# Block sums and token sums of a fused attention and two-layer expert kernel, moved from VectorE to GpSimd

## The chip, the cores and the metric

The kernel runs on one core of a Trainium2 chip. The time is the device time of one execution in microseconds (us), start to end as the runtime measures it. Engines are named as the profile names them: PE is TensorE (PEld its weight loads), DVE is VectorE, ACT is ScalarE, POOL is GpSimd, SP is SyncE, which here only issues DMAs. Every engine works off its own instructions strictly in the order in which they were written for it, and waits for others by semaphores.

## The reference

Attention with a learned position bias over 4 batches, 8 heads, 576 rows and head size 64; its output, 2304 tokens of width 512, goes through two feed-forward stages.

```python
h   = max(max(x @ moe_w1, x @ moe_w2), x @ moe_w3)          # 512 -> 768
x   = h @ moe_w_out                                         # 768 -> 512
out = (sigmoid(x @ w_gate) * (x @ w_val)) @ w_out           # 512 -> 1536 -> 512
```


## The kernel before

All matrices are float32 and are multiplied on PE as pairs of float16 parts: a value f is scaled, its rounded half is the first part, the rest the second, and three products of parts replace one. `halves` writes such a pair: an ACT copy for the first part, and on DVE `scalar_tensor_tensor` (f times scale minus the first part, L1103) for the second. The scale comes from a sum of squares: ACT squares a decoded block (L1117), one small matmul with ones sums it over the partitions (`col_sums`, L566), and DVE makes the scale of it (L1122, L584 to L586). The weights arrive as 64-bit words and are decoded by three DVE instructions (L554 to L556).

The last stage multiplies the tokens by `w_gate` with a seven-product scheme over 2 x 2 blocks. For it, sums and differences of blocks are needed: `pair_weights` makes four sums of the blocks of one sixth of `w_gate` (128 x 256 elements each, one after the other, each but one needing an earlier one), for six sixths i = 0 to 5; `token_sums` makes four sums of the token blocks of one batch (128 x 576 elements each), for four batches. All of them are written by `add2` (L1096), between SBUF buffers, in float32. `add2` serves a third place too, `quad`, where it makes the second float16 part of the gated product. `quad(b, i)` (which first scales its sigmoid's factor, L1263) are the products of batch b with sixth i (PE L1269), `outs` the last products (PE L1325); `moe1` is the first feed-forward stage (PE L945, its maxima on DVE L975, and its own float16 second parts on DVE L987 or on POOL L986).

Nothing of the order is left to the hardware. The program is recorded instruction by instruction (`Recorder.add`), with a cost for each by engine and size (`Recorder.cost`), and `Recorder.emit` then lays the instructions out engine by engine: it takes next what can start earliest by these costs, within four classes of urgency. An instruction recorded on two engines within one `join` goes to the engine where it would end earlier. So a change of one instruction's engine changes its cost in the plan, and with it the order on all engines. The plan knows no work of one engine that slows another.

The stretch that the change touches runs from the end of attention to the first `outs`: at the profile's times, from 540 to about 708 us the weights of the last stage are decoded and split, the tokens of batches 0 and 1 are prepared, and PE runs the last `moe1` and then the first six `quad`s. One block of sums, that of i = 0, is made earlier (412 to 425 us, in attention).

Of the kernel before, what the change touches and what calls it, by code (L numbers as in the profile page):

```python
# [15 lines left out]
ALU = mybir.AluOpType  # L16
# [400 lines left out]
SIDE_H, FIRST_H = (2, 4), (3, 2)  # L417
SIDE_CLS = ATT
EARLY = 120
ADD_POOL = False  # L420
AHEAD = ()
SPLIT5 = True
PE_ALL, PE_SQ = 6, 8
# [30 lines left out]
def tile_kernel(ctx, tc, q, k, v, w1, b1, w2, mw1, mw2, mw3, mwo, gw, vw, ow, xtab, masks, out):  # L454
# [15 lines left out]
    nc = Recorder(tc.nc, {x.tensor.name for x in (junk[:, :], q, k, v, w1, b1, w2, mw1, mw2, mw3, mwo, gw, vw, ow, xtab, masks, out)})  # L470
# [118 lines left out]
    def copy_psum(dst, src, scale=1.0):  # L589

        with nc.join():
            nc.scalar.activation(dst, src, AF.Copy, scale=scale)  # L592
            nc.vector.tensor_scalar(dst, src, scale, None, op0=ALU.mult)
# [23 lines left out]
    for rv in (rvb0, rvb):  # L617
# [25 lines left out]
        op=ALU.mult,  # L643
# [448 lines left out]

    def add2(dst, a, b, op):

        with nc.join():
            nc.vector.tensor_tensor(dst, a, b, op=op)  # L1096
            if ADD_POOL:
                nc.gpsimd.tensor_tensor(dst, a, b, op=op)

    def halves(dst, f, s):  # L1100

# [3 lines left out]
    def pair_weights(i, raw, F, S4, js=(0, 1), step=128, SW=SW):  # L1105
# [18 lines left out]
        for j, f in zip(js, fs):  # L1124
            W, s = SW[i][j], scl_gv[:, 0, i, j:j + 1]
            if j:
                for h in range(2):
                    halves([W[:, 2 * h:2 * h + 2, e] for e in range(2)], f[:, :, 128 * h:128 * h + 128].rearrange("p (o k) f -> p o k f", o=2), s)
                    yield
                continue  # L1130
            t = S4().rearrange("p (o k f) -> p o k f", o=4, k=2)
            a11, a12, a21, a22 = f[:, 0:2, 128:256], f[:, 2:4, 128:256], f[:, 0:2, 0:128], f[:, 2:4, 0:128]
            add2(t[:, 0], a21, a22, ALU.add)
            add2(t[:, 1], t[:, 0], a11, ALU.subtract)
            add2(t[:, 2], a11, a21, ALU.subtract)
            add2(t[:, 3], a12, t[:, 1], ALU.subtract)
            halves([W[:, 0:2, e] for e in range(2)], f[:, :, 128:256].rearrange("p (o k) f -> p o k f", o=2), s)
            yield
            halves([W[:, 2, e] for e in range(2)], a22, s)
            halves([W[:, 3:7, e] for e in range(2)], t, s)  # L1140
            yield
# [114 lines left out]
    def quad(b, i):  # L1256

        h0 = 64 * (b % 2)
        ugm = ug[:, b, i:i + 1]
        sg, XC = sg_r(), XC_[b % 2]  # L1260
        c21, c22, c11, c12 = (sg[:, HS * n:HS * (n + 1)] for n in range(4))
        with nc.at(BIAS):
            nc.vector.tensor_scalar(ugm, scl["gw"][:, 1, i:i + 1], ub[:, b:b + 1], None, op0=ALU.mult)  # L1263

        def group(ps, W, o, x, start, stop):
            with nc.join():
                for kk in range(2):
                    for z, (wp, xp) in enumerate(((0, 0), (0, 1), (1, 0))):
                        nc.tensor.matmul(ps, lhsT=W[:, o, wp, kk], rhs=XC[:, x, xp, kk], start=start and kk == z == 0, stop=stop and kk == 1 and z == 2)  # L1269

        vs = []
        for t, n in enumerate((1, 6, 7, 5, 2, 3, 4)):
            ps = part_r()
            group(ps, SW[i][0], WS[n - 1], n - 1, True, True)
            with nc.at(BIAS):
                if n == 1:
                    copy_psum(c11, ps)
                elif n == 6:
                    nc.vector.tensor_tensor(c12, ps, c11, op=ALU.add)
                elif n == 7:  # L1280
                    nc.vector.tensor_tensor(c21, ps, c12, op=ALU.add)
                elif n == 5:
                    nc.vector.tensor_tensor(c12, ps, c12, op=ALU.add)
                    nc.vector.tensor_tensor(c22, ps, c21, op=ALU.add)
                else:
                    c = {2: c11, 3: c12, 4: c21}[n]
                    nc.vector.tensor_tensor(c, ps, c, op=ALU.add)  # L1287
            if t in (0, 2, 3, 5):
                m, hf = ((1, 0), (1, 1), (0, 0), (0, 1))[(0, 2, 3, 5).index(t)]
                if not hf:  # L1290
                    pv = two_r()
                    vs.append((m, pv))
                for kh in range(2):
                    group(pv[:, hf], SW[i][1], 2 * m + kh, RAW[hf][kh], kh == 0, kh == 1)
        with nc.at(BIAS):
            for m, pv in vs:
                at = sg[:, S * m:S * m + S]
                nc.scalar.activation(at, at, AF.Sigmoid, scale=ugm)  # L1298
                at = at.rearrange("p (a s) -> p a s", a=2)
                nc.vector.scalar_tensor_tensor(at, pv, DOWN2, at, op0=ALU.mult, op1=ALU.mult)  # L1300
        g2 = sg.rearrange("p (m s) -> p m s", m=2)
        m2 = slice(2 * i, 2 * i + 2)
        with nc.at(BIAS):
            for src, hi, lo in ((g2[:, :, 0:512], gm[b % 2][:, 0, m2], gm[b % 2][:, 1, m2]),
                                (g2[:, :, 512:S], gt[:, 0, m2, h0:h0 + 64], gt[:, 1, m2, h0:h0 + 64])):
                nc.scalar.copy(hi, src)
                add2(lo, src, hi, ALU.subtract)

    def out_rows(pr, ct):

# [66 lines left out]
    for b in range(B):  # L1377
        with nc.at(BIAS):
            batch_scale(b)
            out_scales(b)  # L1380
        for i in range(NP2):
            quad(b, i)
            for ct in after[b].get(i, ()):
                outs((b if b % 2 else b - 1) // 2, ct)
            if i == 3 and 0 < b < B - 1:
                next_tokens(b)
        if b == 1:
            po_r = Ring([bank(7), bank(4)])
        for ct in ends[b]:
            outs(b // 2, ct)  # L1390
# [33 lines left out]
```

## Time and profile before

| | before |
|---|---|
| median of 3 runs (lowest, highest) | 1039.08 us (1037.2, 1039.49) |
| the profiled execution | 1040.86 us |
| its span, first to last instruction | 1039.1 us |
| granted TensorE clock, mean | 0.993 |
| PE busy | 993.7 us, 96% of the span |
| DVE busy | 722.9 us, 70% |
| ACT busy | 597.6 us, 58% |
| POOL busy | 120.0 us, 12%, 146 instructions |

The span is what the trace covers; the profiled execution took 1.8 us more than it. Busy shares are averages over stages that differ much: what an engine's idle time is worth depends on where it lies.

### The profile page before, as it was taken

To read this page: it belongs to the slowest core of one execution; us is meant where nothing else is said; L and a number is where in the kernel's file an instruction comes from. 1 tells how busy PE (TensorE), PEld (TensorE's weight loads), DVE (VectorE), ACT (ScalarE), POOL (GpSimd) and SP (SyncE) were. 2 spreads that over 40 slices of the span, in tenths; PEclk is the share of its full clock that TensorE was granted. 3 is DMA by queue.
4 is the path that set the end of the run, shared out by engine and by line. 5 is a ranking of instruction groups with operands and counts; after the bars stand their busy time and mean duration, and the time that the engine had idled before them with its cause. 6 is when DMAs were issued, how large, how long until landed. Compare 5 with 4: busy or idle time off the path is not lost.

```text
span 1039.1 us, 21298 instructions
## 1 busy us (share of the span) xinstructions
PE 993.7 (96%) x8156; PEld 670.1 (64%) x8156; DVE 722.9 (70%) x1869; ACT 597.6 (58%) x1336; POOL 120.0 (12%) x146
## 2 busy tenths in 40 slices
PE   4898999997999999999999999999999999999998
PEld 2344577664666666677677777876666656766653
DVE  5788998976878789958779989996354335532320
ACT  6898986775787777856765565653233124222221
POOL 1022114342112322112100100000000000000000
PEclk9999999998999999999999999999999999999999
DMA  7896767567999999875686233420010001000001
GB/s 222 252 303 226 271 211 174 164 165 143 213 228 261 234 219 250 206 199 128 146 181 188 82 104 116 138 62 11 11 67 11 11 11 66 2 11 22 11 11 41
DMA packets 172242, 139.49 MB, mean 134 GB/s; under 512 B 111852, under 2 KB 151020, under 8 KB 171628
## 3 DMA queue, kind: packets, MB, share of 16 engines
q1 hardware_dynamic: 169476, 128.39, 47.6%
q10 hardware_dynamic: 2664, 9.74, 3.3%
q8 instruction: 64, 1.05, 0.4%
q14 instruction: 38, 0.31, 0.1%
HBM read 94.25 MB, written 21.23 MB: 111 GB/s over the span
## 4 chain that ended last, share of the span: by engine, by line
PE 77%; DVE 9%; DMA 3%; issue 2%; ACT 2%; POOL 2%; SPq 0%; ACTq 0%; POOLq 0%; DVEq 0%
PE ps L1269 22%; PE ps L945 19%; PE ps L1325 13%; PE ps L890 7%; PE ps L831 5%; PE ps L863 5%; DMA am<-am 2%; PE ps L834 2%; PE ps L669 2%; POOL am L858 1%; DVE am L1103 1%; DVE am L847 1%; DVE wm L975 1%; PE ps L566 1%; PE ps L611 1%
## 5 line engine op out<-in xcount | busy, mean ns | idle before, releaser
L945 PE MATMUL ps<-wm 128*128 128x320 f16 (+2 forms) x2304 | 304.9, 286 | 0.2 <-DVE am L975 0.2
L945 PEld LDWEIGHTS <-wm 128*128 128x128 f16 x2304 | 222.9, 99 | 54.9 <-issue 3.2
L1269 PE MATMUL ps<-am 128*128 128x288 f16 x1800 | 223.9, 286 | 1.3 <-DVE wm L1300 0.7
L1269 PEld LDWEIGHTS <-am 128*128 128x128 f16 x1800 | 176.1, 98 | 48.5 <-issue 1.6
L1325 PE MATMUL ps<-wm 128*128 128x512 f16 x648 | 142.5, 379 | 0.0
L848 ACT ACTIVATE am<-am,small 128x576 f32<-128x576 f32 (+1 forms) x160 | 123.1, 770 | 30.3 <-DVE small L847 19.4
L847 DVE CUSTOM_DVE_ANT_0 am<-ps,am 128x576 f32<-128x576 f32 (+1 forms) x160 | 117.9, 749 | 28.2 <-issue 13.0
L1325 PEld LDWEIGHTS <-wm 128*128 128x128 f16 x648 | 63.3, 98 | 73.5
L858 POOL TENSOR_SCALAR am<-am,small 128x576 f32<-128x576 f32 (+1 forms) x65 | 64.5, 997 | 206.1 <-DVE small L850 135.5
L890 PE MATMUL ps<-am 128*64 128x128 f32 (+4 forms) x980 | 81.0, 313 | 1.1 <-DVE wm L896 0.7
L592 ACT ACTIVATE am<-ps 128x512 f32<-128x512 f32 (+3 forms) x146 | 66.1, 472 | 26.9 <-PE ps L863 23.5
L863 PE MATMUL ps<-ident,am 128*128 128x128 f32 x450 | 72.2, 282 | 7.5 <-POOL am L858 6.1
L863 PEld LDWEIGHTS ps<-ident,am 128*128 128x128 f32 x450 | 51.1, 143 | 26.1 <-POOL am L858 10.4
L1298 ACT ACTIVATE x<-x,ug 128x576 f32<-128x576 f32 x24 | 18.6, 775 | 77.8 <-DVE x L1287 77.7
L831 PE MATMUL ps<-am 64*128 64x512 f16 (+1 forms) x390 | 55.1, 384 | 7.3 <-DMA am<-am 6.8
L1333 ACT ACTIVATE x<-ps,uo 128x128 f32<-128x128 f32 x64 | 18.2, 368 | 75.3 <-PE ps L1325 55.4
L1298 ACT ACTIVATE wm<-wm,ug 128x576 f32<-128x576 f32 x24 | 18.5, 771 | 56.8 <-DVE wm L1287 56.8
L890 PEld LDWEIGHTS ps<-am 128*64 128x64 f32 x680 | 39.5, 137 | 17.8 <-issue 4.9
L872 DVE SCALAR_TENSOR_TENSOR am<-am,small 128x576 f16<-128x576 f32 (+1 forms) x60 | 48.0, 825 | 3.9 <-ACT am L871 3.8
L975 DVE SCALAR_TENSOR_TENSOR wm<-ps,small,wm 128x256 f32<-128x256 f32 (+1 forms) x84 | 43.0, 512 | 8.5 <-PE ps L945 6.8
L1269 PE MATMUL ps<-am,x 128*128 128x288 f16 x360 | 46.0, 286 | 2.5 <-DVE am L1103 1.9
L871 ACT ACTIVATE am<-am,small 128x576 f16<-128x576 f32 (+1 forms) x60 | 43.6, 766 | 5.3 <-ACT am L848 2.7
(180 smaller groups left out, 1382.6 us busy)
## 6 DMA issues: line engine op xcount, KB each, us to landing
am<-bias_d SPq DMA_DIRECT2D x49, 576.0 KB, 4.6
bias_d<-am SPq DMA_DIRECT2D x36, 320.0 KB, 4.4
wm<-in_moe_w_dram SPq DMA_DIRECT2D x12, 768.0 KB, 6.2
am<-bias_d ACTq DMA_DIRECT2D x15, 576.0 KB, 4.9
wm<-in_moe_w_out_dram SPq DMA_DIRECT2D x24, 256.0 KB, 2.9
x<-in_moe_w_val_dram SPq DMA_DIRECT2D x20, 256.0 KB, 4.1
x_d<-wm SPq DMA_DIRECT2D x4, 1152.0 KB, 4.7
am<-in_v_dram SPq DMA_DIRECT2D x16, 256.0 KB, 5.7
```

The source lines that it names most:

```text
L592: nc.scalar.activation(dst, src, AF.Copy, scale=scale)
L831: nc.tensor.matmul(s_main[o][:m], lhsT=q_[h, eq], rhs=k_[h, ek, 0:512], start=(i == 0), stop=(i == 2), tile_position=(64 * o, 0))
L847: nc.vector.tensor_tensor_reduce(e[:m, c], S_[o][:m], bt[:m, c], -1.0, 3.0e38, ALU.add, ALU.min, mx[:m])
L848: nc.scalar.activation(e[:m, c], e[:m, c], AF.Exp, scale=-1.0, bias=mx[:m], accum_out=l[:m, o:o + 1])
L858: nc.gpsimd.tensor_scalar(e[:m, c], e[:m, c], r[:m, o:o + 1], 1.0, op0=ALU.mult, op1=ALU.mult)
L863: nc.tensor.transpose(ps[:, t], e[:, 128 * (t0 + t):128 * (t0 + t) + 128], ident)
L872: nc.vector.scalar_tensor_tensor(ph[:m, 1, c], e[:m, c], f, ph[:m, 0, c], op0=ALU.mult, op1=ALU.subtract)
L890: nc.tensor.matmul(ps[64 * o:64 * o + 64, :N], lhsT=vv[:, o, tv], rhs=pp[:, tb], start=(i == j == 0), stop=(i == len(todo) - 1 and j == 4) ...
L945: nc.tensor.matmul(ps, lhsT=W(wp, kk), rhs=X(xp, kk), start=(first and i == 0), stop=(last and i == 2))
L975: nc.vector.scalar_tensor_tensor(hv, ps, f, hv, op0=ALU.mult, op1=ALU.max)
L1269: nc.tensor.matmul(ps, lhsT=W[:, o, wp, kk], rhs=XC[:, x, xp, kk], start=start and kk == z == 0, stop=stop and kk == 1 and z == 2)
L1325: nc.tensor.matmul(po, lhsT=g[:, gi, kk], rhs=OW[:, wi, kk], start=(kk == 0 and i == 0), stop=(kk == K2 - 1 and i == 2))
```

## The change

`add2` writes its one instruction for POOL and no longer for DVE. The sums in `quad` no longer go through `add2`; their line writes for DVE as before (`LO_POOL` is 0, so its condition is never met). Counted over the program, 40 instructions leave DVE for POOL: 24 of 128 x 256 elements (four for each sixth of the gate weights) and 16 of 128 x 576 (four for each batch). One L987 of `moe1` goes from POOL to DVE. The orders on all engines are planned anew. Lines from 421 to 1092 move down by one, lines behind `add2` move up by two (L566 becomes L567, L1103 becomes L1101).

```diff
-ADD_POOL = False
+ADD_POOL = True
+LO_POOL = 0
...
     def add2(dst, a, b, op):
 
-        with nc.join():
-            nc.vector.tensor_tensor(dst, a, b, op=op)
-            if ADD_POOL:
-                nc.gpsimd.tensor_tensor(dst, a, b, op=op)
+        (nc.gpsimd if ADD_POOL else nc.vector).tensor_tensor(dst, a, b, op=op)
...
                 nc.scalar.copy(hi, src)
-                add2(lo, src, hi, ALU.subtract)
+                (nc.gpsimd if LO_POOL > b and src.shape[2] > 64 else nc.vector).tensor_tensor(lo, src, hi, op=ALU.subtract)
```

What stands at the end of POOL's row of the kernel before (am, wm and x are the three SBUF arenas; L858 scales attention weights, L986 belongs to `moe1`; x3 means three of a kind in a row):

```order
L858 TENSOR_SCALAR am<-am,small 128x576
L986 TENSOR_TENSOR wm<-wm 128x576
L858 TENSOR_SCALAR am<-am,small 128x576
L986 TENSOR_TENSOR wm<-wm 128x576
L858 TENSOR_SCALAR am<-am,small 128x576 x3
L986 TENSOR_TENSOR wm<-wm 128x576 x3
```

And from the last attention row on in the changed kernel:

```order
L859 TENSOR_SCALAR am<-am,small 128x576 x3
L1096 TENSOR_TENSOR am<-am 128x576
L1096 TENSOR_TENSOR am<-am 128x2x288 x3
L1096 TENSOR_TENSOR am<-am 128x256 x8
L987 TENSOR_TENSOR wm<-wm 128x576
L1096 TENSOR_TENSOR am<-am 128x256 x8
L987 TENSOR_TENSOR wm<-wm 128x576
L1096 TENSOR_TENSOR wm<-wm 128x256 x4
L1096 TENSOR_TENSOR x<-wm 128x576
L1096 TENSOR_TENSOR wm<-wm 128x2x288 x3
```

POOL, which had three instructions left behind attention, now has the token sums of batch 0, the sums of sixths 1 and 2, an L987, sixths 3 and 4, another L987, sixth 5, and the token sums of batch 1 (those of batches 2 and 3 follow).

DVE at the start of the stretch, before (the token sums of batch 0 and the second parts that use them, then the first decode):

```order
L1103 SCALAR_TENSOR_TENSOR am<-x_75,gv_su,am 128x2x256 x2
L1096 TENSOR_TENSOR am<-am 128x576
L1096 TENSOR_TENSOR am<-am 128x2x288 x2
L1103 SCALAR_TENSOR_TENSOR am<-am,small 128x576 x2
L1096 TENSOR_TENSOR am<-am 128x2x288
L1103 SCALAR_TENSOR_TENSOR am<-am,small 128x576 x4
L554 TENSOR_SCALAR am<-am 128x4x64 x2
L555 SCALAR_TENSOR_TENSOR am<-am 128x4x64 x2
```

And in the changed kernel:

```order
L1101 SCALAR_TENSOR_TENSOR am<-x_75,gv_su,am 128x2x256 x2
L555 TENSOR_SCALAR x_75<-x_75 128x4x64 x2
L556 SCALAR_TENSOR_TENSOR x_75<-x_75 128x4x64 x2
L557 SCALAR_TENSOR_TENSOR x_75<-x_75 128x4x64 x2
L555 TENSOR_SCALAR x_75<-x_75 128x4x64 x2
L556 SCALAR_TENSOR_TENSOR x_75<-x_75 128x4x64 x2
L557 SCALAR_TENSOR_TENSOR x_75<-x_75 128x4x64
L1101 SCALAR_TENSOR_TENSOR am<-am,small 128x576 x2
L557 SCALAR_TENSOR_TENSOR x_75<-x_75 128x4x64
L1101 SCALAR_TENSOR_TENSOR am<-am,small 128x576 x3
L555 TENSOR_SCALAR am<-am 128x4x64 x2
```

Where the token sums stood, DVE now decodes a block of `w_val`; the second parts come behind it.

PE in the last `moe1`, in the changed kernel (L567 is `col_sums`, the small matmul that stands between the squares of a weight block and its scale; L946 are the products of `moe1`):

```order
L946 MATMUL ps<-wm 128x256
L567 MATMUL ps<-small,ones 128x4
L946 LDWEIGHTS wm
L946 MATMUL ps<-wm 128x256
L946 LDWEIGHTS wm
L946 MATMUL ps<-wm 128x256
L946 LDWEIGHTS wm
L946 MATMUL ps<-wm 128x256
L567 MATMUL ps<-small,ones 128x4
```

Before, no two of the eight `col_sums` of this part stand closer than 16 matmuls. Counted in matmuls from the start of PE's order, these two moved from 4148 to 4112 and from 4164 to 4116, and the four that follow from 4237 to 4222, 4340 to 4274, 4419 to 4314 and 4477 to 4420. The `quad`s and `outs` behind them keep their places but for a few short pieces.

## Rows read from the trace of the kernel before

**Rows 1.** The page: DVE's busy tenths in 40 equal slices of the span.

```profile
DVE  5788998976878789958779989996354335532320
```

**Rows 2.** Windows of 25 us: busy PE, PEld, DVE, ACT, POOL; clock, DMA, GB/s.

```profile
550.00:575.00 25.00, 24.00 (x195) 18.67 (x194) 24.31 (x74) 15.22 (x40) 1.28 (x1) 1.00 0.60 175
575.00:600.00 25.00, 23.33 (x192) 18.44 (x191) 24.46 (x71) 13.12 (x37) 3.72 (x2) 1.00 0.30 85
...
675.00:700.00 25.00, 22.84 (x187) 18.01 (x186) 24.90 (x63) 14.01 (x32) 0.00 (x0) 1.00 0.21 64
...
725.00:750.00 25.00, 25.00 (x160) 15.49 (x159) 10.51 (x22) 6.41 (x13) 0.00 (x0) 1.00 0.06 22
```

**Rows 3.** PE's timeline, 540 to 708 us: start, length, count; [idle before, its releaser].

```profile
551.23 0.39 PE L566 MATMUL ps<-small,ones 128*128 128x4 f32 x2 [0.69 <-ACT junk L599]
...
568.13 0.39 PE L566 MATMUL ps<-small,ones 128*128 128x4 f32 x2 [0.31 <-ACT junk L1117]
...
581.74 0.39 PE L566 MATMUL ps<-small,ones 128*128 128x4 f32 x2 [1.11 <-ACT junk L1117]
...
592.25 0.39 PE L566 MATMUL ps<-small,ones 128*128 128x4 f32 x2 [0.56 <-ACT junk L1117]
...
637.68 3.10 PE L1269 MATMUL ps<-am 128*128 128x288 f16 x24 [0.71 <-DVE wm L1300]
...
694.47 3.22 PE L1269 MATMUL ps<-am,x 128*128 128x288 f16 x25 [0.26 <-DVE x L1300]
699.59 3.93 PE L1269 MATMUL ps<-am,x 128*128 128x288 f16 x29 [1.90 <-DVE am L1103]
703.86 1.82 PE L1269 MATMUL ps<-am,x 128*128 128x288 f16 x12 [0.34 <-DVE wm L1281]
706.23 0.90 PE L1269 MATMUL ps<-am 128*128 128x288 f16 x6 [0.55 <-DVE wm L1287]
```

**Rows 4.** Groups by shape on DVE: count, busy us, mean ns.

```profile
L1096 DVE TENSOR_TENSOR am<-am 128x256 f32<-128x256 f32 x16 | 6.0, 412 | 0.0
...
L1096 DVE TENSOR_TENSOR am<-am 128x576 f32<-128x576 f32 x4 | 3.0, 759 | 1.7 <-issue 1.6
```

**Rows 5.** POOL's timeline from 540 to 605 us, all of it.

```profile
560.20 1.28 POOL L986 TENSOR_TENSOR wm<-wm 128x576 f16<-128x576 f32 x1 [52.49 <-ACT wm L984]
578.57 1.69 POOL L986 TENSOR_TENSOR wm<-wm 128x576 f16<-128x576 f32 x1 [17.09 <-ACT wm L984]
589.29 2.03 POOL L986 TENSOR_TENSOR wm<-wm 128x576 f16<-128x576 f32 x1 [9.02 <-ACT wm L984]
```

**Rows 6.** DVE's timeline around those three, and elsewhere for comparison.

```profile
540.01 2.35 DVE L1096 TENSOR_TENSOR am<-am 128x576 f32<-128x576 f32 x3 [1.60 <-issue]
...
551.07 0.28 DVE L554 TENSOR_SCALAR x<-x 128x256 int32<-128x256 int32 x1
...
560.69 0.94 DVE L554 TENSOR_SCALAR am<-am 128x256 int32<-128x256 int32 x1
...
567.40 1.08 DVE L1096 TENSOR_TENSOR am<-am 128x256 f32<-128x256 f32 x3
...
579.18 1.70 DVE L556 SCALAR_TENSOR_TENSOR am<-am 128x256 int32<-128x256 int32 x2
...
590.10 0.47 DVE L975 SCALAR_TENSOR_TENSOR wm<-ps,small,wm 128x256 f32<-128x256 f32 x1
590.50 1.10 DVE L556 SCALAR_TENSOR_TENSOR x<-x 128x256 int32<-128x256 int32 x1
...
592.66 0.41 DVE L556 SCALAR_TENSOR_TENSOR am<-am 128x256 int32<-128x256 int32 x1
```

**Rows 7.** POOL's one-input instructions, two lines: ns shortest/median/longest, and shape.

```profile
L771 POOL TENSOR_SCALAR am<-am,small x48: 522/532/1234, 164.4 to 474.1; 128x320 f16<-128x320 f32 x48
...
L812 POOL TENSOR_SCALAR am<-am,small x10: 789/798/1628, 191.8 to 479.8; 128x640 f16<-128x640 f32 x10
```

**Rows 8.** The chain that ended last, one piece of `moe1`: start, length, count.

```profile
599.88 19.45 PE ps L945 x156
```

## The prediction

> **What bounds the kernel now.** I read the page first: the table of busy times drawn from it (above) has PE at 96% of the span and DVE at 70%. PE is the bound, and the most that any change on another engine can win is PE's idle time. DVE's row of slices [rows 1] shows that its 70% is an average of two halves: eights and nines up to about 700 us, then threes. So I looked next at windows of 25 us. From 725 to 1025 us each of the twelve reads 25.00 busy for PE, with DVE mostly under half busy (the first is shown); in the windows at 550, 575 and 675 us DVE is busy for 24.3 to 24.9 of 25, and PE is not full [rows 2]. What is won or lost must come from there. The sums of the token batches 2 and 3, and most of what else the change moves behind 708 us, lie under a full PE and cost and win nothing; the cover is gone only if a token sum is later by the tens of us for which POOL and DVE are half empty there.
>
> PE's timeline gives the idle time piece by piece [rows 3]. The nine waits make 6.4 us. Three of them, 0.31, 1.11 and 0.56, stand before a `col_sums`: PE waits for ACT's squares, and these for DVE's decode. Four, 1.90, 0.34, 0.55 and 0.26, are waits for DVE in and right behind the first `quad` of batch 1. The other two (0.69 for squares of the attention tokens, 0.71 behind the first sigmoid) are chains in which DVE's load is not the matter. So 5.0 us of PE's time hang on DVE: 2.0 before 600 us, 3.0 around 700.
>
> **What the change takes from DVE there.** 20 of the 24 small sums and 8 of the 16 large ones lie in this stretch. A small sum alone takes 0.41 us [rows 4], but in a row each further one adds (1.08 - 0.41) / 2 = 0.335 [rows 6]: 20 x 0.335 = 6.7. A large one is 0.76, about 0.75 in a row: 8 x 0.75 = 6.0. One L987 comes back to DVE: its float16 difference of 128 x 576 is nearest to the large sums, 0.76. Together 11.9 us less.
>
> **What it puts on POOL, and what that does to DVE.** The trace has POOL adding two SBUF tensors of 576 elements: 1.28, 1.69 and 2.03 us [rows 5]. The reader is to see what DVE did meanwhile. At 560.69 a decode instruction that takes 0.28 elsewhere took 0.94; at 579.18 two L556 took 1.70, where two should take 0.41 + 0.34; at 590.50 one took 1.10, not 0.41 [rows 6]. Each ends just after POOL's instruction does. The L975 at 590.10, which reads PSUM and one SBUF buffer, ran through at 0.47. So a DVE instruction with two SBUF inputs, or this decode, stands still until POOL's has ended: 0.66, 0.95 and 0.69 us, 0.77 in the mean. And POOL, where it comes while DVE is in such instructions, waits first: that is the 0.41 and 0.75 above 1.28.
>
> The Trainium skill says the same in "SBUF — State Buffer", section "Who interferes with whom": a DVE instruction with two SBUF inputs and a GpSimd one that reads SBUF share a port pair, and the second to come "fully blocks" for the whole of the other. The rows agree, down to the instruction that has only one SBUF input and is let through. It speaks against the change: by it, taken to the letter, each sum on POOL would hold DVE for its whole length, which is the second rival below.
>
> So a large sum removes 0.75 from DVE and gives back 0.77. For the small sum POOL has no row. From below: POOL's one-input instruction takes 0.53 for 320 elements and 0.79 for 640, so 0.265 us are fixed [rows 7]; the two-input one then has (1.28 - 0.265) / 576 = 1.76 ns per element, and 256 elements take 0.72. By proportion alone it would be 0.57, and it is hardly more than 1.28, the larger one's time. I take 0.72, since a fixed part is seen. What of it DVE loses is bounded by 0 (it lies under an L975, of which there is one to every two or three decode instructions) and 0.72. The large ones leave 1.28 - 0.77 = 0.51 unblocked; I take the same for the small: 0.21. The sum: 8 x 0.77 + 20 x 0.21 = 10.4, less 0.77 for the L986 that is no longer on POOL: 9.6. By the Trainium skill's "GPSIMD Engine Reference", section "Performance versus the Vector engine", GpSimd takes 1.96 times as long as DVE for an addition of 2048 elements; an estimate by that page would be 0.41 x 1.96 = 0.81 for the small sum, and 1.8 us more on POOL in all; the larger row here gives 1.28 / 0.76 = 1.7.
>
> The sums of a sixth are a chain of four. On DVE it took 1.4 us, on POOL 4 x 0.72 and a wait of about half a us before each: 4.9. Behind it stands `halves` of all four sums, in order on DVE. For sixth 1 the new order leaves 3.5 us of DVE work between the last decode and that instruction, for the others 4.5 to 6. So DVE waits 1.4 us once.
>
> DVE in all: 11.9 taken away, 9.6 + 1.4 = 11.0 given back. It is left 0.9 us lighter, where the plan reckons with 11.9.
>
> **What the new order makes of that.** The plan set `col_sums` earlier, in the belief that DVE is lighter. The seventh of its block went from matmul 4477 to 4420: 57 matmuls at 19.45 / 156 = 0.125 [rows 8], 7.1 us. Up to there DVE loses 4 large sums and 12 small ones (3.0 + 4.0 us) and gets one L987 (0.8), and the 1.6 us in which it stood idle at 540 [rows 6] are filled with the decode that now stands there: 7.8 us, which is the plan's 7.1 and a little. But POOL takes from it 4 x 0.77 + 12 x 0.21 + 2 x 0.77 + 1.4 = 8.5, against 2.3 before: 6.2 more. In the kernel before, 2.3 us of such standstill became 2.0 us of PE waiting. At the same rate 6.2 would be 5.4 us of waiting; DVE's surplus of 0.7 and what slack lies between one `col_sums` and the next takes some of it. Between nothing and 5.4 I take 3.5: more than half, since the three sums waited at were all tight. **+3.5 us.**
>
> In return the waits around 700 us should go. They are for the second parts of batch 1's tokens, eight in a row on DVE. Before, two of them stood ahead of DVE's ninth row L1263 and three ahead of the tenth; now it is four and seven, and PE, being 3.5 us later, waits less for anything. POOL's chain for them is longer, 4 x (1.28 + 0.4) = 6.7 against 3.0, but starts earlier by more than that. Of the 3.05 us I take all but a tenth as gone: **-2.8 us.** The waits of 0.69 and 0.71 stay.
>
> The four sums made at 412 to 425 us: 1.3 us off DVE, 0.8 back, in attention, where POOL's scaling of attention weights now stands behind them by up to 0.7 us each time. PE idles little in that part; I take **-0.2**, between -0.8 and +0.8.
>
> Sum: +3.5 - 2.8 - 0.2 = +0.5 us. The profiled execution took 1040.86 us, 1.8 over its span; the median of the runs is that much lower, 1039.08, and the sum goes on it: 1039.6 us. What a measurement of this kernel can tell from no change is about 0.2%, 2.1 us: this is no change.
>
> **The rivals.**
>
> *Faster: the small sums pass under DVE's PSUM reads.* If a small sum blocks DVE by under 0.1 us and the larger ones by 0.5, up to the seventh sum POOL takes 4 x 0.5 + 12 x 0.1 + 2 x 0.5 = 4.2, no more than 1.9 above what it took before, and DVE's surplus with its slack covers that. Then the 2.0 us before 600 stay, or fall by half, and those around 700 go: -2.8 to -4.8, 1034.3 to 1036.3 us, middle 1035.5. For it: POOL gets in where DVE is at an L975, and an L975 is nearly as long as a small sum holds. Against it: all three large ones blocked for more than half of their length.
>
> *Slower: POOL's sums hold DVE in full.* A small sum that blocks for its whole 0.72 costs DVE twice what it saves: 12 x 0.51 = 6.1 us more up to the seventh sum, and 8 x 0.51 = 4.1 behind it. At a half to 0.86 of this passed on, PE is 3 to 5 us later at 600 and wins back no more there: 1042.6 to 1044.6, middle 1043.5. It decides from about 0.4 us of blocking per small sum, more than the 0.335 that each saves. For it: the chain of four on POOL comes at a time when the order has DVE in decode, one two-input instruction after another. Against it: L975 and the tiny scale instructions come between.
>
> *Slower by a new wait:* DVE, in order, waits at `halves` for POOL's chain of token sums, at 540 or at 680 us. Planned in time, but each of the four may come 0.4 to 0.75 later [rows 5], up to 3 us in all; with all of it on the path the forecast becomes 1042.6. It has part of the chance of the slower side.
>
> *Nothing moves, because DVE's relief lies where PE doesn't wait.* That is 1039.1, inside my forecast.
>
> **Chances.** 0.39 for no change (1037.0 to 1041.2), 0.33 for the faster rival, 0.28 for the two slower ones. The likeliest case's own range is 1037.5 to 1041.5. For 8 in 10 the range reaches half into both others: 1035.0 to 1043.5 us.
>
> **What the changed profile would show.** POOL: about 40 instructions more, small ones near 0.7 us where nothing is in their way, large ones 1.28 to 2.0. DVE: 40 fewer; L555 to L557 and `halves` with some instructions of 1 us and more, about 10 us in all between 540 and 700, so that DVE's busy time there hardly falls. PE: more idle time than 2.0 us before `col_sums` between 550 and 600 us, and nearly none around 700; 25.00 in every window behind 725. The forecast is wrong if DVE's instructions show no standstill beside the small sums (then faster), or if PE's idle time up to 600 us exceeds about 7 us (then slower), or if PE falls idle behind 725 us, where I have put nothing.

## The result

The changed kernel is slower. The first comparison gave 1052.23 us (median of 4; 1050.24 to 1056.4) against 1039.28 for the kernel before, a ratio of 1.0106 (95%: 1.0068 to 1.0143). A second one, with 12 runs, gave 1044.44 (1038.58 to 1053.69) against 1039.44, a ratio of 1.0058 (1.0024 to 1.0093); it is called e8 below. By the ratios it takes some 6 to 11 us more, by the medians 5 to 13 (a ratio compares the single executions and is not the quotient of the two medians). The ratios leave out three executions that were slower than the others of their kernel: 2561.25 us of e5 (the traced one, so its order is read from e11), 3515.16 us of the kernel before beside it and 1045.73 us of e6. The forecast was 1039.6 us, its range 1035.0 to 1043.5.

The page of the profiled execution (1051.09 us), first the engines' busy times, then DVE's 40 slices:

```profile
span 1049.3 us, 21321 instructions
...
PE 998.4 (95%) x8156; PEld 672.8 (64%) x8156; DVE 722.2 (69%) x1829; ACT 598.7 (57%) x1337; POOL 166.3 (16%) x185
...
DVE  5788998976878789868789969996354335632320
```

DVE has 40 instructions fewer and is busy for 722.2 us, where it was 722.9: hardly anything of its load has gone. POOL has 46 us more.

Windows of the changed kernel (columns as in [rows 2]); the first four answer to those rows:

```profile
550.00:575.00 25.00, 22.14 (x169) 17.18 (x169) 22.67 (x67) 14.90 (x44) 5.63 (x7) 0.93 0.62 191
575.00:600.00 25.00, 23.16 (x190) 18.23 (x188) 24.45 (x64) 14.93 (x38) 8.09 (x10) 1.00 0.31 89
675.00:700.00 25.00, 23.49 (x190) 18.31 (x189) 24.69 (x57) 14.70 (x33) 5.02 (x3) 1.00 0.20 64
725.00:750.00 25.00, 25.00 (x158) 15.35 (x157) 7.20 (x18) 4.61 (x12) 0.00 (x0) 1.00 0.06 22
775.00:800.00 25.00, 23.72 (x181) 17.57 (x180) 18.01 (x29) 10.27 (x18) 6.41 (x4) 1.00 0.13 52
875.00:900.00 25.00, 23.64 (x165) 15.98 (x164) 17.74 (x24) 11.84 (x20) 6.42 (x4) 1.00 0.17 59
```

The reader is to see two things: PE is not full in the last two windows, where it was 25.00 before, and each of them holds four instructions of POOL.

PE's timeline has the idle time in pieces, as in [rows 3]. These are all of its waits between 500 and 900 us:

```profile
550.25 4.33 PE L946 MATMUL ps<-wm 128*128 128x288 f16 x36 [1.71 <-ACT wm L593]
557.19 0.39 PE L567 MATMUL ps<-small,ones 128*128 128x4 f32 x2 [2.61 <-ACT junk L600]
...
580.24 0.38 PE L567 MATMUL ps<-small,ones 128*128 128x4 f32 x2 [0.53 <-ACT junk L1115]
...
586.85 0.39 PE L567 MATMUL ps<-small,ones 128*128 128x4 f32 x2 [1.07 <-DVE gv_su L587]
...
600.14 0.39 PE L567 MATMUL ps<-small,ones 128*128 128x4 f32 x2 [0.39 <-ACT junk L1115]
...
626.78 0.39 PE L567 MATMUL ps<-small,ones 128*128 128x4 f32 x2 [1.54 <-ACT junk L1115]
...
645.76 0.39 PE L567 MATMUL ps<-small,ones 128*128 128x6 f32 x2 [0.19 <-ACT junk L1202]
...
679.72 8.24 PE L1267 MATMUL ps<-am 128*128 128x288 f16 x66 [0.21 <-DVE x L1298]
688.12 0.39 PE L567 MATMUL ps<-small,ones 128*128 128x6 f32 x2 [0.16 <-ACT junk L1202]
692.60 10.45 PE L1267 MATMUL ps<-am 128*128 128x288 f16 x84 [1.14 <-DVE wm L1298]
787.66 14.36 PE L1267 MATMUL ps<-am 128*128 128x288 f16 x114 [1.21 <-DVE wm L1282]
894.42 14.24 PE L1267 MATMUL ps<-am 128*128 128x288 f16 x114 [1.36 <-DVE wm L1282]
```

They make 12.1 us against 6.4. Cut into three stages, up to 605 us, 605 to 716, and behind that: 6.31, 3.24 and 2.57 here, 2.67, 3.76 and none before. So PE waits 5.7 us more. That is about the second comparison's 5.0 us. The rest of the 10.2 us by which this execution's span is longer than that of before (1049.3 against 1039.1) lies elsewhere: 2.5 us were there already when the same 108 matmuls of `moe1` began, in the changed kernel (first row) and before (second). The third row is e8, the changed kernel once more, which reached them 1.9 us earlier than the kernel before. So these 2.5 us belong to the execution and not to the change:

```profile
521.95 13.44 PE L946 MATMUL ps<-wm 128*128 128x256 f16 x108
```

```profile
519.44 13.44 PE L945 MATMUL ps<-wm 128*128 128x256 f16 x108
```

```profile
517.54 13.44 PE L946 MATMUL ps<-wm 128*128 128x256 f16 x108
```

And the granted clock of 0.93 between 550 and 575 us costs, as an estimate, 7% of 25, about 1.75 us.

What POOL did, by shape (count, busy us, mean ns, idle before), and its timeline at two places:

```profile
L1096 POOL TENSOR_TENSOR am<-am 128x256 f32<-128x256 f32 x16 | 13.8, 884 | 35.8 <-DVE am L557 22.7 <-ACT wm L593 12.2 <-DVE small L1120 0.8
L1096 POOL TENSOR_TENSOR am<-am 128x576 f32<-128x576 f32 x4 | 9.1, 2282 | 31.3 <-DMA am<-in_moe_w_gate_dram 31.1
...
L1096 POOL TENSOR_TENSOR x<-x 128x256 f32<-128x256 f32 x4 | 2.8, 723 | 5.3 <-DVE x L557 5.3
```

```profile
541.28 9.36 POOL L1096 TENSOR_TENSOR am<-am 128x576 f32<-128x576 f32 x4 [31.06 <-DMA am<-in_moe_w_gate_dram]
...
778.18 1.40 POOL L1096 TENSOR_TENSOR x<-wm 128x576 f32<-128x576 f32 x1 [85.03 <-DMA wm<-x_d]
780.37 5.16 POOL L1096 TENSOR_TENSOR wm<-wm 128x576 f32<-128x576 f32 x3 [0.78 <-DVE am L1101]
```

A small sum with nothing in its way takes 0.72 us, a large one 1.40. The four large ones at 541 us take 9.36 us, not 5.6. On DVE in the same stretch, and behind 775 us:

```profile
541.23 0.75 DVE L556 SCALAR_TENSOR_TENSOR x<-x 128x256 int32<-128x256 int32 x2
541.90 0.75 DVE L557 SCALAR_TENSOR_TENSOR x<-x 128x256 int32<-128x256 int32 x2
...
543.99 3.84 DVE L1101 SCALAR_TENSOR_TENSOR am<-am,small 128x576 f16<-128x576 f32 x2
...
777.46 2.73 DVE L1101 SCALAR_TENSOR_TENSOR am<-wm,small,am 128x576 f16<-128x576 f32 x2 [2.23 <-ACT am L1100]
...
780.55 1.84 DVE L1101 SCALAR_TENSOR_TENSOR am<-wm,small,am 128x576 f16<-128x576 f32 x1 [0.35 <-ACT am L1100]
...
782.68 1.59 DVE L1101 SCALAR_TENSOR_TENSOR am<-wm,small,am 128x576 f16<-128x576 f32 x1
...
784.56 1.59 DVE L1101 SCALAR_TENSOR_TENSOR am<-wm,small,am 128x576 f16<-128x576 f32 x1
...
787.16 0.44 DVE L1282 TENSOR_TENSOR wm<-ps,wm 128x288 f32<-128x288 f32 x1
```

Up to 543.99 DVE runs its decode at full speed and POOL makes no headway; then POOL does, and two second parts (L1101) take 3.84 us where two take 1.55 elsewhere. Behind 775 us a second part takes 0.8 us where nothing is in its way (e12's rows, further down); beside POOL's sums two together took 2.73, and single ones 1.84, 1.59 and 1.59. Back at 541 us, ACT stands behind the same chain, in order:

```profile
547.24 1.44 ACT L1100 ACTIVATE am<-am,small 128x576 f16<-128x576 f32 x2 [2.43 <-POOL am L1096]
549.13 0.78 ACT L1100 ACTIVATE am<-am,small 128x576 f16<-128x576 f32 x1 [0.45 <-POOL am L1096]
549.81 0.39 ACT L593 ACTIVATE wm<-ps 128x288 f32<-128x288 f32 x1
```

The L593 that is late behind it is the one that PE waits for at 550.25.

### The profile page after: what moved, and what is told of

Same layout as the page of the kernel before. It is cut to its first block, busy times and chain, and to the rows that moved or that the text cites. A ratio compares the mean times of both kernels' runs of the same rounds, so it can differ in the third digit from the quotient of the medians.

```text
span 1049.3 us, 21321 instructions
## 1 busy us (share of the span) xinstructions
PE 998.4 (95%) x8156; PEld 672.8 (64%) x8156; DVE 722.2 (69%) x1829; ACT 598.7 (57%) x1337; POOL 166.3 (16%) x185
## 5 line engine op out<-in xcount | busy, mean ns | idle before, releaser
L946 PE MATMUL ps<-wm 128*128 128x320 f16 (+2 forms) x2304 | 307.0, 287 | 3.3 <-ACT wm L593 1.7
L946 PEld LDWEIGHTS <-wm 128*128 128x128 f16 x2304 | 223.9, 99 | 59.5 <-issue 6.1
L593 ACT ACTIVATE am<-ps 128x512 f32<-128x512 f32 (+3 forms) x147 | 66.6, 472 | 27.3 <-PE ps L864 23.7
L772 POOL TENSOR_SCALAR am<-am,small 128x320 f16<-128x320 f32 x48 | 31.5, 673 | 95.2 <-DVE small L767 67.2
```

Of the source, the lines that this page charges most:

```text
L946: nc.tensor.matmul(ps, lhsT=W(wp, kk), rhs=X(xp, kk), start=(first and i == 0), stop=(last and i == 2))
```

## The experiments

Theory: an instruction of POOL that reads two SBUF tensors and a DVE instruction that does (or one of the decode, whose L554 reads a single one and stood still all the same in [rows 6]) keep each other waiting, so that a sum on POOL costs DVE about what it saves, and what is queued behind the sums on ACT and DVE is late. Rivals: the order planned anew costs the time by itself; or POOL is too slow or the hand-over to it is, whatever it does there. The columns in the middle are PE's waits in microseconds, summed from its timeline between 500 and 900 us by the three stages above, as for the changed kernel. DVE is its busy time on the traced execution's page. The time is the median, with the ratio to the kernel before on the same chip. Three chips were used: e1 to e4, e5 to e8 and e9 to e12 have one each, with medians of the kernel before of 1038.84, 1039.44 and 1040.52 us.

| | the 40 sums are on | order | to 605 | to 716 | behind | sum | DVE | us | ratio (95%) |
|---|---|---|---|---|---|---|---|---|---|
| before | DVE | old | 2.67 | 3.76 | 0 | 6.4 | 722.9 | 1039.28 | 1 |
| changed | POOL | new | 6.31 | 3.24 | 2.57 | 12.1 | 722.2 | 1052.23 | 1.0106 (1.0068 to 1.0143) |
| e8 | POOL, as changed | new | 6.29 | 2.74 | 2.76 | 11.8 | 723.0 | 1044.44 | 1.0058 (1.0024 to 1.0093) |
| e1 | 24 small on POOL, 16 large on DVE | its own | 4.29 | 4.09 | 0 | 8.4 | 719.9 | 1039.27 | 1.0002 (0.9972 to 1.0031) |
| e2 | 16 large on POOL, 24 small on DVE | its own | 3.67 | 3.84 | 2.57 | 10.1 | 725.4 | 1043.21 | 1.0031 (1.0006 to 1.0056) |
| e3 | POOL | old | 4.27 | 5.11 | 1.19 | 10.6 | 716.6 | 1046.21 | 1.0044 (1.0008 to 1.0079) |
| e4; e12 | DVE | new | 5.02 | 4.06 | 0 | 9.1 (e12) | 722.7 (e12) | 1044.8 (e4) | 1.0047 (1.0018 to 1.0076) |
| e5; e11 | nothing: POOL writes only | old | 2.12 | 3.49 | 0 | 5.6 (e11) | 706.4 (e11) | 1041.7 (e5) | 1.0004 (0.9973 to 1.0035) |
| e6 | nothing: POOL writes only | new | 0.99 | 1.24 | 0 | 2.2 | 705.5 | 1035.15 | 0.9960 (0.9931 to 0.9990) |
| e9 | nothing: POOL writes as long as a sum | new | 1.23 | 1.56 | 0 | 2.8 | 705.5 | 1038.94 | 0.9977 (0.9949 to 1.0005) |
| e7 | POOL, planned as slow | its own | 5.92 | 4.72 | 0 | 10.6 | 720.9 | 1051.18 | 1.0107 (1.0066 to 1.0149) |
| e10 | 32 on POOL, last 8 large on DVE | its own | 6.29 | 3.33 | 0 | 9.6 | 720.7 | 1043.65 | 1.0033 (1.0004 to 1.0062) |

### Which sums, and which part of the change (e1 to e4)

e1 and e2 put one kind of sum on POOL and plan the order for it:

```diff
-    def add2(dst, a, b, op):
-        (nc.gpsimd if ADD_POOL else nc.vector).tensor_tensor(dst, a, b, op=op)
+    def add2(dst, a, b, op, pool):   # weights: POOL_W, tokens of batch b: b in POOL_T
+        (nc.gpsimd if pool else nc.vector).tensor_tensor(dst, a, b, op=op)
+POOL_W, POOL_T = True, ()            # e1;  e2: False, (0, 1, 2, 3)
```

Expected of e1: 

> The 24 small sums on POOL, the 16 token sums on DVE again, order planned for that. Theory (the token sums are what costs: on POOL they starve behind DVE's two-input instructions, then hold DVE, and DVE waits in order for them): without them the time is within 0.2% to 0.4% of the kernel before, 1038 to 1043 us; PE full behind 725 us; no PE wait of over 1.5 us between 540 and 560 us. Rival (the small sums and the earlier col_sums cost most): 1045 us or more, PE idle before col_sums as in the changed kernel.

Expected of e2: 

> The 16 token sums on POOL, the 24 small sums on DVE, order planned for that. Theory (token sums cost): 1045 to 1050 us, with the two stretches of PE idle time near 785 and 890 us of the changed kernel (1.3 us each) and 3 us or more lost near 545 to 560 us. Rival (small sums cost): under 1042 us.

The small sums on POOL neither win nor lose, the large ones lose, though less than was expected of e2. DVE's busy time says the same: 3.0 us less than before in e1 and 2.5 us more in e2 (one or two L987 changed engine as well, with orders of their own). Both together lose more than the two apart (0.0002 and 0.0031 against 0.0058 and 0.0106), but the intervals allow for a plain sum with e8.

e3 and e4 keep one kernel's order and put the sums on the other's engine: the plan is told one engine, the instruction is written for the other. The lines are e3's; e4 has "POOL" in the first and `nc.nc.vector` in the second.

```diff
-        (nc.gpsimd if ADD_POOL else nc.vector).tensor_tensor(dst, a, b, op=op)
+        nc.add("DVE", "tensor_tensor", (dst, a, b), {"op": op},      # e3: planned for DVE, on POOL
+               lambda: nc.nc.gpsimd.tensor_tensor(dst, a, b, op=op))  # e4: planned for POOL, on DVE
```

Expected of e3: 

> The order is planned as before, with all 40 sums costed and queued as DVE work; each is then issued to POOL instead. No work is left out. Theory (the two engines hold each other, whatever the order): as slow as the changed kernel or slower, 1048 to 1058 us, since the old order has other work queued right behind each sum. Rival (the new order is what costs, by putting col_sums early): within 0.3% of the kernel before, 1036 to 1042 us.

Expected of e4: 

> The order of the changed kernel, planned with the sums as POOL work; each is then issued to DVE at the place that the plan gives it. No work is left out. Theory (the engines hold each other): without POOL's sums most of the loss goes, 1036 to 1044 us, PE full behind 725 us. Rival (the new order costs): 1046 us or more, with DVE short of the time that the plan thought free.

Expected of e12, e4 once more: 

> The kernel of e4 once more, for its trace. Its wait of 3.3 us for a DMA at 508 us was either one of this order (then it comes again) or one of that execution (then PE's waits behind 500 us add up to about 9 us, 2.5 more than before's 6.4).

Each half costs about the same, 1.0044 and 1.0047. Both runs fell between what their theory and their rival allowed. In e3 DVE was relieved: 716.6 us, 6.3 less than before, and against the same order with fills (e11, 706.4, next section) POOL's sums gave back 10.2 us only. So what a sum on POOL costs DVE hangs on the order. The kernel was slower all the same: PE waited 10.6 us, 4.2 more than before. The 3.3 us for a DMA did not come again in e12, so they belong to one execution, and e12's waits are what the table has: 2.7 us more than before. By itself this says only that this order is not good with the sums on DVE; whether it is a bad order the next pair tells.

### POOL without reading (e5, e6, e9, e11)

The 40 sums are left out of the computation; POOL fills their destination with a constant, at the same place in its queue. A fill has no operands to wait for: it waits only for what still uses the buffer that it overwrites. So e9's first fill for sixth 1 waits for a second part (L1108, at 553.39 us), where the changed kernel's first sum waits for the decode (L557, at 557.76).

```diff
-        (nc.gpsimd if ADD_POOL else nc.vector).tensor_tensor(dst, a, b, op=op)
+        nc.add("POOL", "tensor_tensor", (dst, a, b), {"op": op},     # e5: "DVE", the old order
+               lambda: nc.nc.gpsimd.memset(dst, 0.5))                # e9: two fills, two and a half for a large one
```

Expected of e5: 

> The old order of work, as in e3, but each of the 40 sums is replaced by a Pool instruction that only fills the destination with a constant and reads nothing: the sums are left out of the computation, their places, waits and the engine stay. Theory (two-input instructions of Pool and of DVE hold each other up): without operands to read, Pool holds nobody; DVE's busy time falls from 716 us to 705 to 710 us, PE's waits between 540 and 708 us fall under the 6.4 us of before, time 1031 to 1038 us. Rival (the loss is the hand-over to another engine, whatever it does there): as e3, 1043 to 1049 us.

Expected of e6: 

> The changed kernel's order with the same replacement: each of the 40 sums is a Pool instruction that fills its destination and reads nothing, so the sums are left out. Theory (mutual holding up): the token sums no longer starve at 541 to 561 us, the two waits near 785 and 890 us of 1.2 and 1.4 us go, and what is left is what the order costs by itself, 1038 to 1045 us. Rival (the hand-over): the two waits stay and the time is 1047 to 1053 us.

Expected of e9: 

> As e6 (changed order, the sums left out, Pool only fills the destination), but each sum is replaced by two or three fills in a row, so that Pool is taken about as long as by a sum: two fills for a small one, 2 x 0.31 = 0.62 us against 0.72 for a sum alone, two and a half for a large one, 2 x 0.58 + 0.34 = 1.5 us against 1.40. Theory (Pool and DVE hold each other up because both read): Pool is as slow as in the changed kernel but holds nobody, the time stays near e6, 1033 to 1040 us, and PE's waits behind 500 us stay under 5 us. Rival (Pool is simply slow, and what stands behind its chain is late): the waits come back to 8 to 12 us and the time to 1042 to 1048 us.

Expected of e11: 

> The kernel of e5 once more, for its trace (old order, sums left out, Pool only fills): PE's waits between 500 and 740 us add up to 5 to 7 us, about the 6.4 us of before, although DVE's busy time is 11 us less: what PE waits for there is set by the order and by the decoding, not by the sums. Rival: under 3 us, as in e6.

With fills as long as sums (e9), PE's timeline keeps these four waits between 500 and 900 us (its lines behind `add2` stand 7 higher):

```profile
555.82 0.39 PE L567 MATMUL ps<-small,ones 128*128 128x4 f32 x2 [0.25 <-ACT junk L600]
583.08 0.39 PE L567 MATMUL ps<-small,ones 128*128 128x4 f32 x2 [0.98 <-DVE gv_su L587]
622.34 0.39 PE L567 MATMUL ps<-small,ones 128*128 128x4 f32 x2 [1.37 <-ACT junk L1122]
641.32 0.39 PE L567 MATMUL ps<-small,ones 128*128 128x6 f32 x2 [0.19 <-ACT junk L1209]
```

The page's busy times of e9, and below it of e12 (same order, the sums on DVE):

```profile
PE 996.0 (96%) x8156; PEld 671.5 (65%) x8156; DVE 705.5 (68%) x1829; ACT 596.8 (57%) x1337; POOL 155.5 (15%) x241
```

```profile
PE 997.8 (96%) x8156; PEld 672.8 (65%) x8156; DVE 722.7 (69%) x1869; ACT 598.2 (58%) x1337; POOL 118.6 (11%) x145
```

So the 40 sums cost DVE 722.7 - 705.5 = 17.2 us when it makes them, and 722.2 - 705.5 = 16.7 us when POOL does (17.5 by e8's 723.0). POOL's 155.5 - 118.6 = 36.9 us of fills hold nobody, its sums do: the rival of the slow engine falls, since e9's fills take nearly as long as sums alone would (24 x 0.72 + 16 x 1.40 = 39.7). What e9 doesn't copy is the sums' dependence on their operands. DVE's busy time is free of that, since waiting is not counted in it. PE's waits are not: the fills for batch 0 start 15.0 us behind the 108 matmuls of `moe1`, the sums 19.3. PE's waits in the first two stages are 9.55 us in the changed kernel and 2.79 in e9; how much of the difference is the holding up, and how much the earlier start, is therefore not shown. For the last stage the changed kernel's own rows tell it (further down). The Trainium skill, "SBUF — State Buffer", section "Who interferes with whom", has a DVE instruction with two SBUF inputs contend with a GpSimd instruction that reads SBUF, "not with one that only writes it". Both halves of that agree with these runs: 16.7 us for sums that read, nothing for 36.9 us of fills.

The order itself is good for what it was made for: with nobody held it takes 1035.15 us (e6), 4 us under the kernel before and under the 1038 to 1045 that its theory had. With the longer fills it is 1.6 us (e9), which is not clear of none. In the old order the same relief wins nothing (e5: 1.0004; e11's waits 5.6 us, 0.8 less than before), so e5 missed its theory's 1031 to 1038 us, and its rival's 1043 to 1049 too. The reading that the old plan had packed the other work around the sums fits this; no run shows it by itself.

### Planning for it, and the last two batches (e7, e8, e10)

```diff
-        t = {"tensor_tensor": 0.3 + 0.002 * n,
+        t = {"tensor_tensor": 0.3 + (0.005 if "float32" in str(out.dtype) else 0.002) * n,   # e7
...
+POOL_W, POOL_T = True, (0, 1)                                                                # e10, with e1's add2
```

Expected of e7: 

> The changed kernel with one figure of its planner changed: a Pool sum with an f32 result is put down as 0.3 + 0.005 n us (1.58 us for 256 elements, 3.18 us for 576) in place of 0.3 + 0.002 n (0.81 and 1.45), so that what needs a sum is planned later. Theory (much of the loss is DVE, ACT and PE standing in order behind sums that come later than planned): the waits at 541 to 561, 785 and 890 us shrink by 3 to 5 us, 1040 to 1047 us. Rival (the mutual holding up itself costs the time, wherever it is planned): 1047 to 1053 us.

Expected of e8, the changed kernel itself: 

> The changed kernel itself, beside the others on the same chip, as their base. All theories: 1046 to 1053 us, ratio 1.006 to 1.013; the profile again shows a wait of 1.2 to 1.4 us near 785 and near 890 us, and 6 to 9 us for the four token sums at 541 us.

Expected of e10: 

> The changed kernel with the token sums of the last two batches (8 of the 16 large sums) on DVE again, the other 32 sums on Pool, order planned anew. Theory: the two waits of 1.2 to 1.4 us near 785 and 890 us go, everything ahead of 740 us stays, so 2.5 us less than the changed kernel: 1040 to 1046 us, ratio about 1.004. Rival (nothing behind 708 us matters, as the prediction had it): as the changed kernel, ratio 1.006 to 1.010.

e8 came out a little under its 1046 to 1053 us; the waits that it was to show were there, 1.33 and 1.43 us near 782 and 889 us, and its four token sums took 8.66 us.

e10 leaves the first stage as it was (6.29 us in both) and takes the waits behind 716 us away; its windows there:

```profile
775.00:800.00 25.00, 25.00 (x190) 18.32 (x188) 17.42 (x32) 9.80 (x15) 0.00 (x0) 1.00 0.03 12
...
875.00:900.00 25.00, 25.00 (x192) 18.64 (x191) 17.12 (x33) 10.70 (x19) 0.00 (x0) 1.00 0.13 53
```

The ratio of 1.0033 is what the theory said; the waits show the 2.6 to 2.8 us directly, the times alone (1.0033 against e8's 1.0058) would not. In e7 those waits go too, but a `col_sums` near 560 us then waits 3.40 us, the sum stays at 10.6, and the time is no better: planning the sums as slow moves the loss and doesn't take it away. Its 1051.18 us, of 6 runs, is more than its waits account for; that stays open.

## Why the prediction was wrong

**The price of the sums was right in total, in part by luck.** The prediction had a small sum give 0.21 us of standstill back to DVE and a large one 0.77. Over all 40 that is 24 x 0.21 + 16 x 0.77 = 17.4 us; 16.7 and 17.5 were measured. That DVE's busy time hardly falls was said, and held. The two prices were off in opposite directions. DVE has the same 1829 instructions in the same order in the changed kernel and in e9; taken one against the other, those beside the 16 large sums are 4.5 + 2.4 + 3.7 + 3.7 us longer, 0.9 a sum, and those beside the 24 small ones 3.4 us, 0.14 a sum (in e8 0.9 and 0.17). And the total is one of this order: in the old one, e3, it was 10.2. The small sum was put at 0.72 us on POOL and took 0.72, the large one at 1.28 and took 1.40. The 1.4 us for which DVE was to wait at `halves` for a chain of small sums did not come: DVE waits for none of the 40 sums. (Nor do the four make a chain of four: only the second and the fourth need an earlier one.) The rows of before do not agree "down to the instruction that has only one SBUF input": of the three that stood still in [rows 6], L554 has only one as well.

**Up to 605 us, +3.5: the size came out, the step to it failed.** The waits grew by 6.31 - 2.67 = 3.6 us. But the prediction had them at the three `col_sums` behind 560 us, at the rate at which "2.3 us of such standstill became 2.0 us of PE waiting", and these stayed as they were: 0.53, 1.07 and 0.39 make 1.99, before 1.98 [rows 3]. All of the growth lies at 550 and 557 us: PE waits 1.71 for the PSUM copy L593 queued on ACT behind POOL's token sums, and 2.61 where it was 0.69. The forecast had no wait for the token sums at 540, and put the 0.69 down as staying. In the rival that had one, the step that failed is "each of the four may come 0.4 to 0.75 later": the four took 9.36 us, 3.8 more than 4 x 1.40, since DVE's decode stood in one piece in front of them. There it was DVE that waits; ACT waited first, 2.43 us. In e12, with no sums on POOL, the second of the two waits is still 2.43, and with fills (e9) 0.25: this order with the load of the sums is enough for most of it, whichever engine makes them. The 1.71 came in the three runs that have POOL's sums in the changed kernel's order up to there (the changed kernel, e8, e10), and not in e12. That 3.6 lies so near to 3.5 is not evidence for the rate; PE came later to the three `col_sums`, and whether they would have been waited at longer otherwise, no run tells.

**Around 700 us, -2.8: the late token waits went, others came.** The four waits of [rows 3] behind 694 us, 3.05 us, are all gone, as forecast, and so is the 0.71 that was to stay. The changed kernel's five waits between 605 and 716 us are others: the last of them, 1.14, stands behind 456 matmuls of the `quad`s, those of before behind 558 to 624. They make 3.24 us (2.74 in e8), and the sum had nothing for them. The largest, 1.54 (0.64 in e8), is a `col_sums` at 627 us that nobody waited at before; with fills it is 1.37 (e9), so most of it is no matter of the sums. In front of it DVE waits for the DMAs of a block of `w_val`, 1.72 and 0.52 us here, 1.26 in e8, 2.01 and 0.86 in e9; before, such waits of 0.77 and 0.35 reached no `col_sums`. The stage as a whole wins 0.5 to 1.0 us. The error is that one wait was followed through the new order and new ones were put at nothing.

**Behind 708 us, nothing: this step failed plainly.** The prediction said that the sums of batches 2 and 3 "lie under a full PE and cost and win nothing", with cover of "the tens of us for which POOL and DVE are half empty there". They cost 2.57 us (2.76 in e8), and nothing with e10. The prediction had named PE's falling idle behind 725 us as a sign that it is wrong. The empty time of an engine is little cover when its queue is in order: the second parts L1101 stand in DVE's queue between the additions L1277 to L1282 that empty PSUM for PE. The rows of e12, where DVE makes the four sums itself between these, and of e9 below them, where POOL fills (L1108 and L1289 are its L1101 and L1282), show the price:

```profile
770.48 1.55 DVE L1101 SCALAR_TENSOR_TENSOR am<-wm,small,am 128x576 f16<-128x576 f32 x2 [2.19 <-ACT am L1100]
...
776.54 0.81 DVE L1101 SCALAR_TENSOR_TENSOR am<-wm,small,am 128x576 f16<-128x576 f32 x1
...
779.03 0.45 DVE L1282 TENSOR_TENSOR wm<-ps,wm 128x288 f32<-128x288 f32 x1
```

```profile
771.12 1.55 DVE L1108 SCALAR_TENSOR_TENSOR am<-wm,small,am 128x576 f16<-128x576 f32 x2 [2.19 <-ACT am L1107]
...
778.35 0.45 DVE L1289 TENSOR_TENSOR wm<-ps,wm 128x288 f32<-128x288 f32 x1
```

From the first L1101 to the L1282 that PE waits for, DVE takes 778.35 - 771.12 = 7.23 us with fills on POOL, and 779.03 - 770.48 = 8.55 with the four sums among its own work; PE waits in neither. In the changed kernel, without the sums, it takes 787.16 - 777.46 = 9.70: the second parts stand still for 1.18, 1.02, 0.78 and 0.78 us, more than the sums' own 4 x 0.75. That is 1.15 us more than in e12, and PE's wait there is 1.21. So this place hid the 1.32 us by which e12 is over e9, and not the 2.47 of the changed kernel. Only 0.35 of the 9.70 us is waiting, so here it is the holding up that makes L1282 late, and not a sum that comes late.

**The sum.** The middles of the two outer rivals are 1035.3 and 1043.6, not 1035.5 and 1043.5, which moves nothing. +3.5 - 2.8 - 0.2 = +0.5 was forecast; the waits say +3.6 - 0.5 + 2.6 = +5.7 (e8: +3.6 - 1.0 + 2.8 = +5.4), and e8's time +5.0. About half of the miss is the last stage and half the middle one. The four sums at 412 to 425 us, put at -0.2, were not told apart. What the first comparison has above that, 1.0106 against 1.0058, is not explained beyond the two parts of its profile named above.

## What to carry to other kernels

Work moved to another engine relieves the first only if the two can run at the same time: make a version whose moved instructions do nothing but take the time, and one with the sums on the old engine in the new order, and the busy time of the relieved engine tells whether it was relieved (here 705.5 against 722.2 and 722.7 us). It doesn't tell the kernel's time: in e3 DVE had 6.3 us less to do than before, and the kernel was slower. A planner that doesn't know of the holding up spends the relief in advance: its order wants to be judged with the sums that it will get. And a half-empty engine that works in order hides only what fits ahead of the instruction that the full engine waits for, here 1.32 us and not 2.47.

## What had not been expected of the hardware

- The holding up goes both ways, and the one that is in a row of two-input instructions keeps going: a large sum on POOL took up to 4.06 us (its line's longest; 1.40 alone) while DVE's decode ran at its usual 0.75 us for two. The line's answer for POOL:

```profile
L1096 POOL TENSOR_TENSOR am<-am x20: 725/904/4056, 541.3 to 601.4; 128x256 f32<-128x256 f32 x16, 128x576 f32<-128x576 f32 x4
```

- POOL's fills of 36.9 us in all left DVE's busy time as it was with fills of less than half that length (e6 and e9 both 705.5 us).
- The granted clock fell to 0.93 between 550 and 575 us, that is, for a part of that window to 1.2 GHz, behind two waits of PE of 1.71 and 2.61 us. It was 0.93 in the same window of e10 too, behind waits of 1.70 and 2.61. In e8 the same two waits, 1.70 and 2.60, which end there at 545.84 and 552.78 us, passed without it:

```profile
525.00:550.00 25.00, 23.30 (x203) 18.25 (x201) 21.95 (x44) 15.57 (x40) 8.42 (x4) 1.00 0.53 135
550.00:575.00 25.00, 21.87 (x181) 17.35 (x180) 24.23 (x73) 15.46 (x42) 8.75 (x9) 1.00 0.73 216
```

So the waits alone don't decide it; what else does, no run here shows.
